# Moving the tiles that a matmul-bound kernel streams 128 bytes further on in SBUF

## Chip, cores and metric

One Trainium2 chip, one of its cores. The metric is the device time of one execution in microseconds (us): the median of the runs, beside one profiled execution whose span and trace are read below.

## What is computed

The input `x` has 4 sequences of 4096 tokens with 192 channels. A causal convolution of 7 taps runs over each channel (the taps are a softmax over `weight`, one row for each of 8 groups of channels), and its output goes through two feed-forward blocks of width 2048:

```python
a = conv(x, softmax(weight))                    # 16384 x 192
h = a @ w_in;   y = (h * cos(h)) @ w_out        # 192 -> 2048 -> 192
h = y @ w_in2;  g = h * clip(h + 3, 0, 6) / 6
out = g @ w_out2                                # 16384 x 192
```

## The kernel before

Everything is transposed: channels lie on the partitions, tokens along the free dimension. The tokens are cut into 32 blocks of 512 (`NB`, `N`), the width of 2048 into 16 chunks of 128 (`NJ`). One step `t` is one layer, one block and one chunk: `steps` lists 1024 of them.

To keep the precision of float32 with one-pass matmuls, every operand is split into a high part (rounded to `F32R`) and a remainder. A product is then three matmuls, high by high, high by low and low by high. `mm1` (line 622) makes `h` for two chunks at once: 9 products, each as two matmuls of 64 rows, one on partitions 0 to 63 and one on 64 to 127, which run side by side. Such a couple is called a pair below. `middle` (line 648) turns `h` into the activation and splits it into `gh` and `gl`; `mm2` (line 691) multiplies these by the second weights into the sums `a` and `b`, 5 pairs a step, one of them with 64 columns of weights only (`half_wide`, line 239). In all 9728 pairs run, 19456 of the 19564 matmul records. The other records are a warm-up in bfloat16 (line 767) and some of the convolutions, which run as float32 matmuls with diagonal weights (lines 484 and 500).

Every matmul loads its own weights, so a weight load (LDWEIGHTS) goes with each. Its **stationary** operand is a slice of `w0` or `w1`, the weights of a layer, which stay in SBUF throughout. Its **moving** operand, 512 columns of float32, is a half of `own`, `swap` or `last` (split input of a layer) or all of `gh` or `gl`.

The order of the work is a schedule computed ahead of the launch (`Schedule.place`) from costs and due times in the code; nothing in it depends on an address.

Where a tile lies follows from the pools, which stand one behind another in SBUF: `wpool` (the weights), `cpool` (constants and the diagonals), `raw_p` (weights being unpacked), `x_p`, `g_p`. Within a pool the tiles stand in the order in which the program first asks for them. In `x_p` that is `xb` (once), `xa` (twice), then `ta`, `tb`, `yb`, four `last`, four `own`, four `swap`, `ya`, `u`; in `g_p` it is `k`, `r`, `gh`, `gl`. The width of the first three is set by two constants, although only 518 columns of each are used:

```python
WIDE_A, WIDE_B = 520, 528                                       # line 43
v.data = new(v, x_p, F32, (P, WIDE_A))[:, : N + PAD]            # line 412, xa
v.data = new(v, x_p, F32, (P, WIDE_B))[:, : N + PAD]            # line 422, xb
```

With these widths the built program has these starts (bytes along a partition):

| tile | start | rest modulo 256 |
|---|---|---|
| `w0`, `w1` | 16512, 65664 | 128 |
| `diag0`, `diag1` | 114880, 118464 | 192 |
| `xb` | 134784 | 128 |
| `xa`, first and second | 136896, 138976 | 192, 224 |
| `last`, first of four | 147200 | 0 |
| `own`, first of four | 163584 | 0 |
| `swap`, first of four | 179968 | 0 |
| `gh`, first of four | 212736 | 0 |
| `gl`, first of four | 220928 | 0 |

All slices that the pairs take of a weight (512, 768, 1024 or 1536 bytes apart) and of a moving tile (2048 bytes apart) are whole multiples of 256 bytes from its start, so each of the 9728 pairs has moving operands with rest 0 and weights with rest 128.

Of the kernel before, what the change touches and what calls it, by code (L numbers as in the profile page):

```python
# [39 lines left out]
NW = 2 * D  # L40


WIDE_A, WIDE_B = 520, 528

UNBIAS_ON_ACT = 32
CAST_ON_ACT = 32
# [802 lines left out]
```

## Time and profile before

| | |
|---|---|
| median of 3 runs | 2318.5 us (2316.7 to 2319.52) |
| the profiled execution's own time | 2316.11 us |
| its span in the trace | 2314.3 us |
| granted TensorE clock, mean | 0.999 |
| PE busy | 2302.1 us, 99% of the span |
| PEld (weight loads) busy | 2066.3 us, 89% |
| DVE, ACT, POOL busy | 1729.7, 1688.6, 1412.2 us (75, 73, 61%) |

PE is TensorE's matmul, PEld its weight load, which overlaps with it. A matmul record lasts from its first column to its modelled end, so records overlap, and "PE busy" alone does not say how fast pairs follow one another. That is read from how many records start in a stretch of time, or from the starts in the timeline.

### The profile page before, as it was taken

How to read it: one execution, taken by the hardware profiler on the slowest of the kernel's cores; microseconds unless marked ns; L12 is line 12 of the kernel's file. 1: busy time of each engine (PE TensorE's matmuls, PEld its weight loads, DVE VectorE, ACT ScalarE, POOL GpSimd, SP SyncE). 2: the span in 40 equal slices, each digit the busy share in tenths (PEclk: the TensorE clock that was granted, in tenths of full speed). 3: DMA queues.
4: the chain of work that ended last, by engine and by line, in shares of the span. 5: the costliest groups of instructions: out<-in, count | busy, mean ns of one | idle time of the engine just before them, and what ended most of it. 6: DMA issues, size and time to landing. Idle time of an engine off the chain costs nothing.

```text
span 2314.3 us, 49748 instructions
## 1 busy us (share of the span) xinstructions
PE 2302.1 (99%) x19564; PEld 2066.3 (89%) x19564; DVE 1729.7 (75%) x2318; ACT 1688.6 (73%) x2977; POOL 1412.2 (61%) x1049
## 2 busy tenths in 40 slices
PE   9999999999999999999999999999999999999998
PEld 4888899999999999999999999999999999999998
DVE  8898976877768777678777778777687776875553
ACT  5998677776777777777767777777777677777675
POOL 2666666666656666666666666666666665665555
PEclk9999999999999999999999999999999999999999
DMA  5322211111101111101111011111011110111000
GB/s 150 84 67 54 55 41 26 45 40 28 44 19 38 40 33 40 37 20 40 39 38 35 26 31 44 38 31 40 18 44 40 30 43 22 26 35 33 17 22 14
DMA packets 39130, 90.91 MB, mean 39 GB/s; under 512 B 6256, under 2 KB 12400, under 8 KB 38896
## 3 DMA queue, kind: packets, MB, share of 16 engines
q1 hardware_dynamic: 38896, 87.74, 14.7%
q8 instruction: 153, 2.51, 0.4%
q14 instruction: 81, 0.66, 0.1%
HBM read 25.32 MB, written 12.58 MB: 16 GB/s over the span
## 4 chain that ended last, share of the span: by engine, by line
PE 98%; DVE 1%; ACT 0%; DMA 0%; SPq 0%; issue 0%; DVEq 0%; ACTq 0%
PE h L636 46%; PE a L705 31%; PE b L705 10%; PE b L242 10%; PE h L500 1%; DMA raw<-w 0%; ACT r L663 0%; ACT da L311 0%; DVE w L262 0%; DVE last L262 0%; ACT w L257 0%; DVE r L666 0%; DVE swap L262 0%; DVE swap L259 0%; ACT k L655 0%
## 5 line engine op out<-in xcount | busy, mean ns | idle before, releaser
L262 POOL TENSOR_TENSOR gl<-r,gh 128x512 fp32r<-128x512 f32 x1024 | 1396.5, 1377 | 866.3 <-ACT gh L257 772.6
L705 PE MATMUL a<-gh,w 64*128 64x512 f32 x4096 | 904.3, 392 | 0.2 <-DVE w L262 0.2
L636 PE MATMUL h<-own,w 64*128 64x512 f32 x3072 | 877.6, 392 | 0.7 <-ACT own L257 0.7
L636 PE MATMUL h<-swap,w 64*128 64x512 f32 x3072 | 665.1, 392 | 3.4 <-DVE swap L259 1.9
L705 PE MATMUL b<-gh,w 64*128 64x512 f32 x2048 | 666.2, 393 | 0.0
L242 PE MATMUL b<-gl,w 64*64 64x512 f32 x2048 | 662.9, 390 | 0.0
L705 PE MATMUL a<-gl,w 64*128 64x512 f32 x2048 | 662.7, 389 | 0.0
L705 PEld LDWEIGHTS a<-gh,w 64*128 64x128 f32 x4096 | 594.7, 185 | 65.5 <-ACT da L311 0.8
L257 ACT ACTIVATE gh<-r 128x512 fp32r<-128x512 f32 x1024 | 619.5, 631 | 32.4 <-DVE r L666 25.5
L636 PEld LDWEIGHTS h<-own,w 64*128 64x128 f32 x3072 | 568.0, 185 | 33.7 <-ACT own L257 1.5
L675 ACT ACTIVATE r<-h,three 128x512 f32<-128x512 f32 x512 | 324.8, 684 | 361.2 <-PE h L636 327.9
L636 PE MATMUL h<-last,w 64*128 64x512 f32 x3072 | 570.7, 391 | 0.0
L660 DVE SCALAR_TENSOR_TENSOR r<-k,h 128x512 f32<-128x512 int32 x512 | 334.9, 682 | 253.5 <-ACT k L655 134.3
L636 PEld LDWEIGHTS h<-swap,w 64*128 64x128 f32 x3072 | 489.6, 185 | 31.6 <-DVE swap L259 2.2
L678 DVE SCALAR_TENSOR_TENSOR r<-r,h 128x512 f32<-128x512 f32 x512 | 327.7, 679 | 219.1 <-ACT r L675 218.8
L636 PEld LDWEIGHTS h<-last,w 64*128 64x128 f32 x3072 | 407.8, 185 | 29.8
L655 ACT ACTIVATE k<-h 128x512 int32<-128x512 f32 x512 | 280.6, 594 | 171.8 <-PE h L636 171.1
L705 PEld LDWEIGHTS a<-gl,w 64*128 64x128 f32 x2048 | 375.9, 185 | 20.3 <-issue 0.8
L705 PEld LDWEIGHTS b<-gh,w 64*128 64x128 f32 x2048 | 376.2, 185 | 18.9 <-DVE tb L739 0.6
L666 DVE TENSOR_TENSOR r<-r,h 128x512 f32<-128x512 f32 x512 | 339.1, 684 | 52.1 <-ACT r L663 51.8
L663 ACT ACTIVATE r<-r,half_pi 128x512 f32<-128x512 f32 x512 | 353.7, 721 | 24.5 <-DVE r L660 23.6
L242 PEld LDWEIGHTS b<-gl,w 64*64 64x64 f32 x2048 | 268.3, 132 | 19.8
(70 smaller groups left out, 1123.7 us busy)
## 6 DMA issues: line engine op xcount, KB each, us to landing
swap<-own SPq DMA_DIRECT2D x126, 256.0 KB, 3.7
last<-last SPq DMA_DIRECT2D x64, 256.0 KB, 3.1
xa<-xa SPq DMA_DIRECT2D x32, 259.0 KB, 2.7
outT<-ta SPq DMA_DIRECT2D x32, 256.0 KB, 2.0
raw<-w SPq DMA_DIRECT2D x16, 384.0 KB, 3.3
xb<-xb SPq DMA_DIRECT2D x16, 259.0 KB, 2.6
raw<-w SPq DMA_DIRECT2D x32, 128.0 KB, 2.7
outT<-u SPq DMA_DIRECT2D x32, 128.0 KB, 2.3
```

The costliest lines, as they stand in the source:

```text
L242: pe.add_instruction(mybir.InstMatmult(name=nc.get_next_instruction_name(), engine=mybir.EngineType.PE, start_tensor_calc=False, stop_tens ...
L257: nc.scalar.activation(out=out, in_=in_, func=AF.Copy)
L262: (nc.vector if e == "dve" else nc.gpsimd).tensor_tensor(out, a, b, op=ALU.subtract)
L500: nc.tensor.matmul(y.data, lhsT=tap(i), rhs=x.data[:, i : i + N], start=(i == 0), stop=(i == TAPS - 1),)
L636: nc.tensor.matmul(h.data, lhsT=w[HALF[i], pw, c * P : (c + 1) * P], rhs=moving[i][c][HALF[i], px], start=(n == 0), stop=(n == len(passes) ...
L655: nc.scalar.activation(out=new(k, g_p, I32), in_=h.data, func=AF.Copy, bias=0.25, scale=1.0 / TWO_PI)
L660: nc.vector.scalar_tensor_tensor(new(r, g_p, F32), k.data, TWO_PI, h.data, ALU.mult, ALU.subtract)
L663: nc.scalar.activation(out=r.data, in_=r.data, func=AF.Sin, bias=half_pi, scale=-1.0)
L666: nc.vector.tensor_tensor(r.data, r.data, h.data, op=ALU.mult)
L675: nc.scalar.activation(out=new(r, g_p, F32), in_=h.data, func=AF.Relu, bias=three, scale=1.0)
L678: nc.vector.scalar_tensor_tensor(r.data, r.data, 6.0, h.data, ALU.min, ALU.mult)
L705: nc.tensor.matmul(out[i].data, lhsT=w_i, rhs=g.data[HALF[i]], **flags)
```

## The change

`xb` becomes 32 columns, 128 bytes, wider. The columns are not used; they push all that stands behind `xb` in `x_p` and `g_p` 128 bytes further on.

```diff
-WIDE_A, WIDE_B = 520, 528
+WIDE_A, WIDE_B = 520, 560
```

After it `own`, `swap`, `last`, `gh` and `gl` start with rest 128 modulo 256, as the weights do. `xb` and everything ahead of it stay. The instructions on each engine and their order are the same in both programs.

## Rows read from the trace of the kernel before

**Rows 1.** The page: busy time of each engine, and the granted clock in 40 slices.
```profile
PE 2302.1 (99%) x19564; PEld 2066.3 (89%) x19564; DVE 1729.7 (75%) x2318; ACT 1688.6 (73%) x2977; POOL 1412.2 (61%) x1049
PEclk9999999999999999999999999999999999999999
```
**Rows 2.** The page: the chain of work that ended last, by engine.
```profile
PE 98%; DVE 1%; ACT 0%; DMA 0%; SPq 0%; issue 0%; DVEq 0%; ACTq 0%
```
**Rows 3.** What PE waited for (engine line, awaited, us in total, times, longest).
```profile
PE h L636 <- DVE swap L259: 1.9, 1, 1.9
PE h L767 <- DVE w L796: 1.3, 1, 1.3
```
**Rows 4.** Stretches from 100 us on: length, busy us and count by engine, clock, DMA, GB/s.
```profile
100.00:500.00 400.00, 400.00 (x3444) 355.83 (x3442) 329.66 (x454) 307.70 (x550) 259.92 (x192) 1.00 0.20 51
500.00:1000.00 500.00, 500.00 (x4307) 456.72 (x4305) 377.05 (x482) 363.47 (x637) 309.68 (x227) 1.00 0.14 34
1000.00:1500.00 500.00, 500.00 (x4308) 456.75 (x4306) 381.74 (x489) 364.36 (x639) 310.43 (x227) 1.00 0.14 35
1500.00:2000.00 500.00, 500.00 (x4308) 456.83 (x4306) 379.39 (x488) 365.13 (x640) 309.69 (x227) 1.00 0.14 34
2000.00:2314.00 314.00, 308.39 (x2655) 281.18 (x2651) 175.35 (x247) 214.99 (x376) 183.62 (x140) 1.00 0.09 23
```
**Rows 5.** Timeline of PE: the bfloat16 warm-up (start us, us, engine, line, operation, count).
```profile
4.10 3.83 PE L767 MATMUL h<-w 128*128 128x512 bf16 x17
```
**Rows 6.** One line's instructions, 1000 to 1500 us: weight loads, ns min/median/max.
```profile
L636 PEld LDWEIGHTS h<-own,w x680: 184/184/188, 1000.5 to 1500.0; 64*128 64x128 f32 x170
...
L242 PEld LDWEIGHTS b<-gl,w x454: 131/131/135, 1002.8 to 1499.5; 64*64 64x64 f32 x152
```
**Rows 7.** Timeline of PE, 1016.90 to 1022.40 us.
```profile
1016.94 0.40 PE L705 MATMUL b<-gh,w 64*128 64x512 f32 x1
...
1017.18 0.39 PE L705 MATMUL a<-gl,w 64*128 64x512 f32 x1
...
1017.41 0.39 PE L242 MATMUL b<-gl,w 64*64 64x512 f32 x1
...
1018.35 0.39 PE L636 MATMUL h<-own,w 64*128 64x512 f32 x1
...
1018.58 0.40 PE L636 MATMUL h<-own,w 64*128 64x512 f32 x1
...
1018.82 0.39 PE L636 MATMUL h<-own,w 64*128 64x512 f32 x1
...
1020.91 0.39 PE L705 MATMUL a<-gh,w 64*128 64x512 f32 x1
...
1021.60 0.39 PE L705 MATMUL a<-gl,w 64*128 64x512 f32 x1
...
1022.05 0.39 PE L705 MATMUL a<-gh,w 64*128 64x512 f32 x1
...
1022.28 0.42 PE L705 MATMUL a<-gh,w 64*128 64x512 f32 x2
```
**Rows 8.** Timeline of the weight loads inside that stretch.
```profile
1018.35 0.18 PEld L636 LDWEIGHTS h<-own,w 64*128 64x128 f32 x1
1018.38 0.18 PEld L636 LDWEIGHTS h<-swap,w 64*128 64x128 f32 x1
1018.58 0.18 PEld L636 LDWEIGHTS h<-own,w 64*128 64x128 f32 x1
```
**Rows 9.** Weight loads by group, 1016.93 to 1017.18, then 1020.90 to 1022.30 us (busy, mean ns).
```profile
L705 PEld LDWEIGHTS a<-gl,w 64*128 64x128 f32 x1 | 0.2, 188 | 0.0
...
L705 PEld LDWEIGHTS a<-gh,w 64*128 64x128 f32 x6 | 0.8, 184 | 0.1
```
**Rows 10.** Timeline of PE: the convolution of `xb` with `diag1`, then of `xa` with `diag0`.
```profile
39.52 6.28 PE L500 MATMUL h<-xb,diag 128*128 128x512 f32 x14
...
46.63 6.28 PE L500 MATMUL h<-xa,diag 128*128 128x512 f32 x14
```

## The prediction

> **What bounds the kernel now.** I read the busy times and the granted clock first. PE is busy for 2302.1 of 2314.3 us and the clock stands at its upper level, 2.4 GHz, in all 40 slices [rows 1]. The chain that ended last is 98% PE [rows 2], and the list of waits says that PE hardly ever stood still for anybody: its longest wait in the whole run is 1.9 us, and the next 1.3 us [rows 3]. So the time is the number of matmul pairs times the spacing of pairs, plus a start of some 100 us in which the first weights and blocks arrive.
>
> The spacing comes from the stretches. Between 1000 and 1500 us 4308 matmul records start [rows 4], which is 2154 pairs, 232.1 ns each; the other stretches give the same. From 100 us to the end the counts are 3444 + 4307 + 4308 + 4308 + 2655 = 19,022 records, **9511 pairs** [rows 4]. Each nanosecond of the spacing is therefore worth 9.5 us of the run.
>
> Is 232.1 ns all streaming? The bfloat16 warm-up has the same 512 columns: 17 records in 3.83 us, of which the last lasts 0.38, so (3.83 - 0.38) / 16 = 215.6 ns each [rows 5]. A pair thus spends 16.5 ns more than columns alone ask for, and it is these 16.5 ns that an address could touch. They are not constant. In the timeline the first halves of eight consecutive pairs start between 1016.94 and 1018.82 us, 235 ns apart, and some 2 us later those of six pairs start between 1020.91 and 1022.28, 228.3 ns apart [rows 7]. The pair at 1016.94 is followed after 0.24 us, and the two between 1021.60 and 1022.05 take 0.225 each, to the timeline's 10 ns. Same kind of instruction, same clock, no wait. Something inside TensorE's reads varies, and there is one trace of it: a weight load takes 184 ns and now and then 188, one of 64 columns 131 and now and then 135 [rows 6], and the load that ran beside the long pair at 1016.94 is one of 188 ns [rows 9]. Weight load and matmul get in each other's way there.
>
> **The change part by part.** No instruction is added, removed or reordered. Three things move.
>
> *The moving operands of all 9728 pairs.* They start 128 bytes apart from the weights modulo 256 before, and 0 apart after. I work out what that does if the two reads disturb each other when they stand at the same rest modulo 256. The next weight load starts with the matmul: matmul at 1018.35, load at 1018.35; at 1018.58 both again [rows 7, 8]. Halving the columns shortens a load by 184 - 131 = 53 ns [rows 6], so a column of weights takes 0.83 ns and 128 of them are read in 107 ns, 4.8 bytes a ns on each partition. The matmul reads 2048 bytes in some 216 to 232 ns, 8.8 to 9.5 bytes a ns. It gains 4 to 4.7 bytes a ns on the load: one lap of 256 bytes in 55 to 64 ns. Before, the load starts half a lap ahead; it is overtaken after about 30 ns and again after about 85 to 95 ns, twice within its 107 ns. After, the two start level, the matmul draws ahead, and it comes round once, after 55 to 64 ns; the second lap would end at 109 ns or later, when the load has read all. One meeting fewer in each pair, if the start itself is not one.
>
> What a meeting costs stands in no row by itself. Bounds: all 16.5 ns could be such meetings, and all could go (215.6 ns a pair: 16.5 x 9511 = 157 us less); or the start becomes a third meeting and all pairs are as long as the one at 1016.94 (240 ns: 7.9 x 9511 = 75 us more). Two meetings in 16.5 ns would be 8 ns each, so that one fewer would give 224 ns. I take less, **228 ns**, because six pairs in a row already run at that spacing today [rows 7], with loads of 184 ns that were not lengthened [rows 9]: it is a speed that the trace shows, where 224 is a division. The gain is (232.1 - 228) x 9511 = **39 us**.
>
> *`xa` and the tiles of the other engines.* `ta`, `yb`, `k`, `r` and the rest move together by the same 128 bytes, so their places to one another stay. DVE and ACT are busy for 381.74 and 364.36 of 500 us [rows 4]; if PE needs 2% less time they stand at 78 and 74%, and POOL at 63%. That cover remains, and I cost them at nothing; without it, 2% longer operations there would still be hidden behind PE. The transfers into these tiles have the same number and size; the DMA share is 0.14 [rows 4]. What would be late next is nothing that I can name.
>
> *The matmuls of the convolutions.* They are 84 of 19,564 records, and lie ahead of 52 us; nothing.
>
> The sum: 2316.1 us for the profiled execution, less 39, is 2277. The median of the runs lies 2.4 us above the profiled execution, so I predict **2279 us**.
>
> **The rivals.**
>
> *Slower: level at the start is the worst place.* Matmul and load begin within 10 ns of each other [rows 7, 8]. With equal rests they then ask for the same place at once, every time, and if the matmul does not draw ahead at once, the start is a meeting that no phase can avoid. It decides from the point at which a pair's average meetings go above today's, that is when the collision at the start costs more than the meeting that falls away. If every second pair became long, as in the stretch from 1016.94 to 1018.82, the spacing would be 235: 2.9 x 9511 = 28 us more, 2346 us. If all did: 240 ns, 2394 us. For it: loads of 188 ns do go with a long pair [rows 9]. Against it: beside the pair at 1017.18 runs a load of half as many columns, that of line 242 for the pair at 1017.41, and it takes 0.23 us like the mean [rows 7]. So the cost now seems to sit in the first half of a load, where the meeting after 30 ns is, and this one goes.
>
> *No change: the addresses do not matter.* Before, two convolutions run with different distances: `xb` with rest 128 against a diagonal with 192, and `xa` (its first buffer) with rest 192 against 192, which is the level case. Both take 6.28 us for 14 records [rows 10]. That is the same to 10 ns, on the same engine. Against it: these are float32 matmuls over all 128 rows, at 0.43 us or so a record, with one load in that time where the pairs have one in 0.23; they may leave room that the pairs do not have. The 16.5 ns could belong to this type of matmul. Then the time stays at 2318.5 us. The Trainium skill says so as a rule ("SBUF — State Buffer", section Who interferes with whom): TensorE has two read ports that are independent, one for the moving operand and one for weight loads, and it never waits on anyone. By that rule the sum is zero; the load of 188 ns beside the long pair is where this trace does not agree.
>
> *The change does not do what it says.* Only what stands behind `xb` moves. The starts of the tiles say that it does for all five moving tiles, so this is left with next to nothing and is counted with no change.
>
> **How the numbers follow.** About 0.2% (4.6 us, half a nanosecond a pair) is what a measurement of this kernel can tell from no change. Faster: 0.57, because the meetings are in the trace and the count of them falls; its own range is 2230 us (223 ns a pair) to 2310 (231). No change: 0.19. Slower: 0.24, most of it between 2325 and 2350 us, the rest up to 2394. The likeliest is faster, at 2279. The range reaches from 2230, below which I leave some 0.08 (towards the bound of 215.6 ns, 2162 us), to 2348, above which some 0.11 is left.
>
> **What would show it.** Right: 1000 to 1500 us holds about 4386 matmul records (500 us over 228 ns, twice) at a clock of 1.00, PE's waits stay at a few us, loads of 188 ns get rare, and the whole gain is spread evenly over the run from 100 us on. The rival of the level start: fewer than 4308 records there, the median load above 184 ns. No change: 4308 within 10. The prediction is wrong if the spacing goes up, or if it goes down and a wait of PE on DVE or ACT gives it back.

## The result, and the profile after

The changed kernel takes **2283.77 us** (median of 4 runs, 2283.35 to 2284.76), the kernel before 2317.6 us in the runs beside it (2316.41 to 2319.52). The ratio is 0.9854, 95% interval 0.9837 to 0.9871: 33.8 us less. Forecast were 2279 us, with a range from 2230 to 2348. The profiled execution took 2284.76 us, with a span of 2283.0 us, against 2314.3 before.

The page of the changed kernel, busy times and granted clock, answers to [rows 1]:

```profile
PE 2271.2 (99%) x19564; PEld 2033.0 (89%) x19564; DVE 1725.4 (76%) x2318; ACT 1689.7 (74%) x2977; POOL 1411.3 (62%) x1049
...
PEclk9999999999999999999999999999999999999999
```

PE is still busy for all but 12 us of the span. A digit 9 of the clock says that a slice, some 57 us, had 90% or more of the upper level of 2.4 GHz on average, as in the kernel before; that the upper level held in the bulk of the run is read from the stretches below, at 1.00. No instruction went away: 19,564 matmul records, as before. The chain that ended last answers to [rows 2], and the list of what PE waited for to [rows 3] (engine line, awaited, us in total, times, longest):

```profile
PE 98%; DVE 1%; ACT 1%; issue 0%; POOL 0%; DVEq 0%; POOLq 0%; ACTq 0%
```

```profile
PE h L636 <- DVE swap L259: 1.8, 1, 1.8
PE h L767 <- DVE w L796: 1.3, 1, 1.3
```

The two longest waits are the same two, within 0.1 us. So the gain came out of no wait, and no new one took it back. It is in how fast pairs follow one another, and that is read from the stretches, which answer to [rows 4]; the first 100 us stand here too (length, then busy us and count of PE, PEld, DVE, ACT, POOL, clock, DMA share, GB/s):

```profile
0.00:100.00 100.00, 94.45 (x545) 59.31 (x547) 86.85 (x162) 71.47 (x137) 37.45 (x38) 0.97 0.40 114
100.00:500.00 400.00, 399.68 (x3492) 341.42 (x3490) 332.70 (x458) 311.53 (x557) 264.25 (x195) 1.00 0.20 51
500.00:1000.00 500.00, 500.00 (x4374) 426.88 (x4372) 382.87 (x494) 371.77 (x651) 313.68 (x230) 1.00 0.14 35
1000.00:1500.00 500.00, 500.00 (x4375) 436.53 (x4372) 382.76 (x493) 370.56 (x649) 314.50 (x231) 1.00 0.14 35
1500.00:2000.00 500.00, 500.00 (x4374) 492.40 (x4373) 382.23 (x493) 369.72 (x646) 315.28 (x231) 1.00 0.14 34
2000.00:2283.00 283.00, 277.02 (x2421) 276.49 (x2417) 157.94 (x220) 194.64 (x340) 166.16 (x128) 0.99 0.10 25
```

The count of PE is what matters. Between 1000 and 1500 us 4375 records start where 4308 did: 2187.5 pairs, 228.6 ns each, where they had 232.1. The three stretches of 500 us agree to one record, so the gain is even over the run. Times the 9511 pairs of the prediction, (232.13 - 228.57) x 9511 = 33.8 us, which is the difference of the medians. The two profiled executions differ by a little less, 31.3 us of span; the first 100 us are part of that, since 545 records start there after the change and 559 before, seven pairs or 1.6 us. The clock is not the same in that start: from 25 to 30 us the granted share was 0.50 (the lower level, 1.2 GHz) after the change, with 22 records, and 0.71 before, with 33. The whole stretch before the change:

```profile
0.00:100.00 100.00, 93.74 (x559) 58.93 (x561) 86.48 (x163) 72.95 (x140) 38.88 (x38) 0.98 0.41 115
```

PEld's busy time says nothing here: 426.88, 436.53 and 492.40 us go with one and the same spacing. Loads of the two halves overlap, and where they overlap more, their union is shorter.

A line's weight loads between 1000 and 1500 us (ns min/median/max), to be laid beside [rows 6]:

```profile
L636 PEld LDWEIGHTS h<-own,w x690: 182/184/185, 1001.9 to 1498.9; 64*128 64x128 f32 x173
...
L242 PEld LDWEIGHTS b<-gl,w x460: 131/131/132, 1000.1 to 1499.8; 64*64 64x64 f32 x154
```

The longest loads of these two groups have gone, 188 to 185 and 135 to 132 ns; the median stays.

The timeline of PE (start us, us, engine, line, operation, operands, number of records merged into the row), at the start of a `mm1` and at the start of the `mm2` behind it, answers to [rows 7]:

```profile
1002.16 0.61 PE L636 MATMUL h<-own,w 64*128 64x512 f32 x2
...
1003.75 0.62 PE L636 MATMUL h<-last,w 64*128 64x512 f32 x4
1004.20 0.39 PE L705 MATMUL a<-gl,w 64*128 64x512 f32 x1
1004.21 0.39 PE L636 MATMUL h<-last,w 64*128 64x512 f32 x1
```

`mm1` has nine pairs. The first half of its first one starts at 1002.16, that of the first pair of `mm2` at 1004.20: 2.04 us, 227 ns a pair. Means over the starts of all first halves, from the 800th to the 9300th pair, tell the two products apart: `mm1` went from 232.4 to 226.85 ns, `mm2` from 232.25 to 230.5. With 4608 pairs of the one and 5120 of the other that is 25.6 + 9.0 = 34.6 us, three quarters of it in `mm1`. In what follows "spacing of `mm1`" and "of `mm2`" are these means.

### The profile page after: what moved, and what is told of

It reads as the page before. It is cut to its first block, busy times and chain, and to the rows that moved or that the text cites. A ratio compares the mean times of both kernels' runs of the same rounds, so it can differ in the third digit from the quotient of the medians.

```text
span 2283.0 us, 49748 instructions
## 1 busy us (share of the span) xinstructions
PE 2271.2 (99%) x19564; PEld 2033.0 (89%) x19564; DVE 1725.4 (76%) x2318; ACT 1689.7 (74%) x2977; POOL 1411.3 (62%) x1049
## 4 chain that ended last, share of the span: by engine, by line
PE 98%; DVE 1%; ACT 1%; issue 0%; POOL 0%; DVEq 0%; POOLq 0%; ACTq 0%
PE h L636 45%; PE a L705 30%; PE b L242 12%; PE b L705 10%; PE h L500 1%; PE h L767 0%; PE h L484 0%; ACT k L655 0%; ACT gh L257 0%; DVE r L666 0%; DVE r L660 0%; ACT r L663 0%; DVE da L322 0%; DVE swap L259 0%; DVE swap L262 0%
## 5 line engine op out<-in xcount | busy, mean ns | idle before, releaser
L636 PE MATMUL h<-own,w 64*128 64x512 f32 x3072 | 862.2, 387 | 0.7 <-ACT own L257 0.7
L705 PE MATMUL b<-gh,w 64*128 64x512 f32 x2048 | 658.8, 390 | 0.0
L705 PE MATMUL a<-gl,w 64*128 64x512 f32 x2048 | 654.9, 386 | 0.3 <-POOL gl L262 0.3
L636 PE MATMUL h<-swap,w 64*128 64x512 f32 x3072 | 651.9, 387 | 3.0 <-DVE swap L259 1.8
L705 PEld LDWEIGHTS a<-gh,w 64*128 64x128 f32 x4096 | 602.7, 184 | 53.6 <-DVE ta L739 1.0
L257 ACT ACTIVATE gh<-r 128x512 fp32r<-128x512 f32 x1024 | 621.5, 630 | 32.4 <-DVE r L666 25.6
L636 PE MATMUL h<-last,w 64*128 64x512 f32 x3072 | 560.1, 386 | 0.0
L636 PEld LDWEIGHTS h<-swap,w 64*128 64x128 f32 x3072 | 478.3, 185 | 37.2 <-DVE swap L259 2.1
```

Source lines behind the costliest of these rows:

```text
L257: nc.scalar.activation(out=out, in_=in_, func=AF.Copy)
L636: nc.tensor.matmul(h.data, lhsT=w[HALF[i], pw, c * P : (c + 1) * P], rhs=moving[i][c][HALF[i], px], start=(n == 0), stop=(n == len(passes) ...
L705: nc.tensor.matmul(out[i].data, lhsT=w_i, rhs=g.data[HALF[i]], **flags)
```

## The experiments

All were timed beside the kernel before on the same chip, which took 2316.4 to 2316.6 us each time. "Distance" is the start of the weights less that of the moving operand, modulo 256: 128 before, 0 after. Each fence holds the stretch from 1000 to 1500 us in the columns of the view above; the count of PE, the first in brackets, gives the spacing (1000 us over the count).

### Whose address is it?

The theory: the distance of moving operands to weights, in which the two reads meet. The rivals: the absolute place of the moving tiles, or that of the tiles of the other engines that moved along.

**1. Weights moved by 128 bytes as well**, and so everything behind them (against the kernel before, with `xb` as wide as it was there). `own`, `swap`, `last`, `gh`, `gl` and all other tiles behind `xb` lie where the change has them, but the distance is 128 again.

```diff
+pad = wpool.tile([P, 32], F32, tag="pad", name="pad")
 W = [wpool.tile([P, NJ, 2, NW], F32R, tag=f"w{l}", name=f"w{l}") for l in range(2)]
```

> The weights and everything behind them lie 128 bytes further on than in the kernel before, so that the moving operands lie exactly where the changed kernel has them (own at 163712), but half a lap of 256 bytes from the weights again. If the distance between the two operands decides: as before, 2318 us, 4308 records from 1000 to 1500 us. If the place of the moving operands themselves, or of the tiles of the other engines, decides: as the change, 2284 us, 4375 records.

```profile
1000.00:1500.00 500.00, 500.00 (x4308) 443.91 (x4306) 381.87 (x489) 364.33 (x640) 310.07 (x227) 1.00 0.14 35
```

2316.32 us, ratio 1.0 (0.999 to 1.0009), and 4308 records, the very count of before. The whole gain is gone.

**2. Only the weights moved.** `xb` gets 8 columns less and two small scratch tiles are saved, so that `own`, `gh` and the rest stay at the addresses of before; weights at rest 0, moving operands at rest 0 (against the kernel before).

```diff
-WIDE_A, WIDE_B = 520, 528
+WIDE_A, WIDE_B = 520, 520
...
-half_pi = cpool.tile([P, 1], F32, tag="half_pi", name="half_pi")
-three = cpool.tile([P, 1], F32, tag="three", name="three")
+both = cpool.tile([P, 2], F32, tag="both", name="both")
+half_pi, three = both[:, :1], both[:, 1:]
...
+pad = wpool.tile([P, 32], F32, tag="pad", name="pad")
...
-kf, sm = t("skf", I32), t("ssum", m=1)
+kf, sm = k, t("ssum", m=1)
```

> Only the weights move by 128 bytes; own, swap, last, gh and gl stay where the kernel before has them (own at 163584), and so do all tiles of x_p and g_p but xb. Distance 0 modulo 256. If the distance decides: as the change, 2284 us. If the place of the moving operands or of the other engines' tiles decides: as before, 2318 us.

```profile
1000.00:1500.00 500.00, 500.00 (x4374) 497.77 (x4372) 382.16 (x492) 370.57 (x650) 315.39 (x231) 1.00 0.14 35
```

2283.83 us, 0.9857 (0.9843 to 0.9872): the whole gain, with no moving tile touched.

**3. The same without the pad** (against experiment 2): weights where they were, moving operands 128 bytes to the other side, 256 bytes below those of the change.

```diff
-pad = wpool.tile([P, 32], F32, tag="pad", name="pad")
```

> The moving operands lie 128 bytes further back instead of further on (own at 163456); the weights stay. Distance 0 modulo 256, but 256 bytes from that of the change modulo 512. If the lap is 256 bytes long: as the change, 2284 us. If it is 512 bytes or longer: another time, 2318 us or something beyond either; the distances of both kernels modulo 512 would then already have differed among the weights' own slices, so I give this little chance.

```profile
1000.00:1500.00 500.00, 500.00 (x4374) 441.12 (x4372) 382.16 (x492) 370.54 (x650) 315.18 (x231) 1.00 0.14 35
```

2283.55 us, 0.9859 (0.9844 to 0.9874). 128 bytes down do what 128 bytes up do, as a period of 256 wants it. Together the three settle whose address it is: experiment 1 against the change, and experiment 2 against before, differ in the distance, and the time follows the distance each time. By rests modulo 256 of weights and moving operands, 128 and 128 (the change) and 0 and 0 (experiment 2) are fast, 128 and 0 (before) and 0 and 128 (experiment 1) are not.

**4. Only `gh` and `gl` moved**, the operands of `mm2` (against the kernel before). If each pair paid for its own distance alone, the pairs of `mm2` would give their share and `mm1` nothing.

```diff
-WU = {}
+WU, pad = {}, g_p.tile([P, 32], F32, tag="pad", name="pad", bufs=1)
```

> Only gh and gl (the pairs of the second product, 5120 of 9728) lie 128 bytes further on; own, swap and last stay. If each pair gains by its own distance, in equal parts: 34 us x 5120/9728 = 18 us, 2300 us. If the gain of a pair depends on what the pairs before left behind: less or more than that, and the other half of the change makes up the rest. If the gain came from the split inputs alone: 2318 us.

```profile
1000.00:1500.00 500.00, 500.00 (x4316) 406.32 (x4314) 382.72 (x491) 365.30 (x641) 311.06 (x227) 1.00 0.14 35
```

2312.1 us, 0.9982 (0.9973 to 0.9991): 4 us, a quarter of what an equal share of all pairs would be. `mm1` stands at 232.6 ns, `mm2` at 231.2; the 230.5 that `mm2` has in the change it does not reach with the same distance. That is a first sign that a pair's spacing hangs on the pairs around it too.

### Do laps explain it? The other distances

The prediction counted how often the matmul's read meets the load's read: twice at distance 128, once at 0. That makes forecasts for the distances between. All four runs change the width of `xb` alone, against the kernel before; experiments 5 and 6 have the distance 32 and 64, experiments 7 and 8 go past level to 224 and 192. The width of `xb` is 552 in experiment 5, as shown, and 544, 568 and 576 in the next three.

```diff
-WIDE_A, WIDE_B = 520, 528
+WIDE_A, WIDE_B = 520, 552
```

> xb is 552 columns wide, so the weights lie 32 bytes ahead of the moving operands modulo 256 (before: 128, change: 0). By laps: the matmul gains 4 to 4.7 bytes a ns, overtakes the load after 7 to 8 ns and again after 61 to 72 ns, both inside the 107 ns of the load: two meetings as before, 2318 us. If nearness to the change's place is enough: 2284 us or little above.

> xb is 544 columns wide: the weights lie 64 bytes ahead. By laps: overtaken after about 15 ns and 75 ns, two meetings, 2318 us. If the time changes evenly with the distance: half way, 2301 us.

> xb is 568 columns wide: the weights lie 32 bytes behind the moving operands. By laps: the matmul is ahead, comes round after 48 to 56 ns and again after 102 to 120 ns, when the load has read all or nearly all: one meeting, and none at the start, so 2284 us or less. If only the level place is good: 2300 us or more.

> xb is 576 columns wide: the weights lie 64 bytes behind (192 ahead). By laps: the matmul comes round after 41 to 48 ns and again after 95 to 112 ns, so one meeting and often a second: between 2284 and 2318 us.

Experiment 5, distance 32:

```profile
1000.00:1500.00 500.00, 500.00 (x4301) 491.13 (x4300) 381.42 (x487) 363.20 (x637) 310.06 (x227) 1.00 0.14 35
```

Experiment 6, distance 64:

```profile
1000.00:1500.00 500.00, 500.00 (x4288) 401.05 (x4286) 380.95 (x486) 360.92 (x633) 309.20 (x226) 1.00 0.14 35
```

Experiment 7, distance 224:

```profile
1000.00:1500.00 500.00, 500.00 (x4292) 454.67 (x4290) 381.17 (x486) 361.57 (x634) 309.74 (x227) 1.00 0.14 35
```

Experiment 8, distance 192:

```profile
1000.00:1500.00 500.00, 500.00 (x4374) 438.31 (x4372) 383.32 (x493) 370.64 (x649) 315.41 (x231) 1.00 0.14 35
```

| distance | layout | median, us | ratio (95%) | spacing of `mm1`, `mm2`, ns |
|---|---|---|---|---|
| 0 | the change | 2283.77 | 0.9854 (0.9837 to 0.9871) | 226.85, 230.5 |
| 32 | experiment 5 | 2320.22 | 1.0015 (1.0006 to 1.0025) | 233.0, 232.5 |
| 64 | experiment 6 | 2325.99 | 1.0041 (1.0027 to 1.0055) | 233.5, 233.15 |
| 128 | before | 2316.4 to 2317.6 | 1 | 232.4, 232.25 |
| 192 | experiment 8 | 2284.33 | 0.9862 (0.9848 to 0.9877) | 228.9, 228.7 |
| 224 | experiment 7 | 2325.4 | 1.0038 (1.0023 to 1.0053) | 233.4, 233.0 |

The laps fall with experiment 7: at 224 they left one late meeting, and wanted 2284 us or less. It took 2325.4. Two distances are good, 0 and 192, and the one between them is among the worst. The spacing of `mm1` and `mm2` also shows that 0 and 192 are not the same state: the totals agree, the shares do not.

The weight loads of experiment 6, to be laid beside [rows 6]:

```profile
L636 PEld LDWEIGHTS h<-own,w x678: 183/184/185, 1000.5 to 1498.4; 64*128 64x128 f32 x170
```

The slowest layout of all has no load of 188 ns either. Of 7604 loads of 128 columns between the 800th and the 9300th pair, 950 last 187 ns or more before (one in eight, and the pairs beside which they run take 240.8 ns on average), none do in the change, and none in experiment 6. So lengthened loads mark one of the slow patterns. They do not measure the loss: the other pairs of the kernel before take 231.3 ns on average, so the long loads go with about 1 of the 3.5 ns.

### Distance alone?

**9. Distance 0, at another place**: weights and moving operands both 32 bytes further on (against the changed kernel).

```diff
+pad = wpool.tile([P, 8], F32, tag="pad", name="pad")
 W = [wpool.tile([P, NJ, 2, NW], F32R, tag=f"w{l}", name=f"w{l}") for l in range(2)]
```

> The weights lie 32 bytes and the moving operands 160 bytes further on than in the kernel before: distance 0 as in the change, but both 32 bytes off the multiples of 64 on which all fast kernels so far have their moving operands. If the distance alone decides: as the change, 2284 us. If the two slower runs at 32 bytes ahead and behind were slow because the moving operands lay at 32 modulo 64: slower, 2320 to 2326 us like those.

```profile
1000.00:1500.00 500.00, 500.00 (x4374) 413.15 (x4372) 382.05 (x493) 370.55 (x649) 315.18 (x231) 1.00 0.14 35
```

2284.06 us, 0.9853 (0.9839 to 0.9868), with the spacings of the change to 0.01 ns. Four layouts have the distance 0 by now, and lie within 0.6 us.

**10. The best of both**: `mm1` at distance 0 as in the change (226.85 ns), `mm2` at 192 as in experiment 8 (228.7 ns). If the spacings add up, it beats both (against the changed kernel).

```diff
-WU = {}
+WU, pad = {}, g_p.tile([P, 16], F32, tag="pad", name="pad", bufs=1)
```

> own, swap and last at distance 0 as in the change, where the trace shows the pairs of the first product at 226.9 ns; gh and gl at 64 bytes behind (weights behind), where the pairs of the second product take 228.7 ns against 230.5 in the change. If a pair's spacing is set by its own distance: 4608 x 226.9 + 5120 x 228.7 against 4608 x 226.9 + 5120 x 230.5 ns, 9 us less than the change, 2275 us, faster than both kernels. If it also hangs on the pairs before it (half of the change, gh and gl alone, gave 4 us where its share was 18): 2284 us or more.

```profile
1000.00:1500.00 500.00, 500.00 (x4356) 413.30 (x4354) 383.46 (x494) 369.75 (x649) 313.52 (x230) 1.00 0.14 36
```

2292.83 us, 0.9892 (0.9878 to 0.9907): 9 us slower than the change, where it was to be faster. `mm2` stayed at 230.5, and `mm1`, whose weights and moving tiles lie at the very addresses of the change, went to 229.0. That is (229.0 - 226.85) x 4608 = 9.9 us, all that was lost.

The trace shows where in `mm1` it was lost. The starts of the first halves of its first pair, its sixth, and the first pair of the `mm2` behind it:

```profile
1010.66 0.39 PE L636 MATMUL h<-own,w 64*128 64x512 f32 x1
...
1011.82 0.39 PE L636 MATMUL h<-swap,w 64*128 64x512 f32 x1
...
1012.73 0.39 PE L705 MATMUL a<-gl,w 64*128 64x512 f32 x1
```

Five pairs take 1.16 us, 232 ns each; the last four take 0.91 us, 227 ns each. Over 390 `mm1` that follow an `mm2` directly, the first five pairs take 230.6, 235.4, 228.7, 231.7 and 230.2 ns on average and each of the last four 226.7, the pace of the change. Where an `mm1` follows another `mm1` (56 of them), all nine positions lie between 226.7 and 227.6. A pair's spacing therefore hangs on the distance in the pairs before it as well as on its own, and at this distance the disturbance is gone after five pairs.

### Is it the length of the load?

**11. Fewer weight columns at the distance of before**: seven of the nine pairs of `mm1` load 32 columns in place of 128, and leave out the rest of their products (against the kernel before). If the load's reads are what costs, less to read costs less.

```diff
                 for i, h in enumerate(hs):
+                    if n % 8:
+                        half_wide(h.data[:32], w[HALF[i], pw, c * P : c * P + 32], moving[i][c][HALF[i], px])
+                        continue
```

> The layout of the kernel before, but 7 of the 9 pairs of the first product load only the first 32 columns of their weights and add to the first 32 rows of h alone, so most of the three-part product is left out. The load then reads for 27 ns instead of 107, and by laps the matmul overtakes it after 30 ns at the earliest, so never. If the loads cause all that a pair takes above 215.6 ns: those 3584 pairs at 216, 232.4 - 216 = 16 ns x 3584 = 59 us less, 2259 us. If they cause only what the change took away and the rest belongs to this type of matmul: 226 to 227 ns there, about 21 us less, 2296 us. If the loads have nothing to do with it: 2317 us.

```profile
1000.00:1500.00 500.00, 500.00 (x4302) 397.16 (x4300) 381.58 (x487) 363.74 (x637) 310.38 (x227) 1.00 0.14 35
```

Its short loads, of line 242, in the same stretch:

```profile
L242 PEld LDWEIGHTS h<-own,w x565: 102/104/108, 1002.1 to 1498.3; 64*32 64x32 f32 x189
```

The loads are shorter by 184 - 104 = 80 ns, and the time is 2319.37 us, 1.0009 (1.0 to 1.0019). `mm1` moves by half a nanosecond (231.9), `mm2` loses one (233.2).

**12. The same at distance 0** (experiment 11 with the width of the change).

```diff
-WIDE_A, WIDE_B = 520, 528
+WIDE_A, WIDE_B = 520, 560
```

> The changed kernel with the same narrow loads: 7 of the 9 pairs of the first product load 32 columns of weights only and add to 32 rows of h, most of the three-part product is left out. With narrow loads the layout of before stayed at 2319 us, so laps are out. If the effect of the distance sits in the first 32 columns of a load, near its start: 2284 us, give or take 5, as with whole loads. If it needs the rest of the load: the gain of the first product (4608 pairs, 232.4 to 226.9 ns, 25 of the 34 us) is lost for 7 of 9 pairs, 2300 us or more.

```profile
1000.00:1500.00 500.00, 500.00 (x4330) 355.23 (x4328) 384.22 (x494) 368.16 (x646) 310.75 (x228) 1.00 0.14 36
```

2305.61 us, 0.9953 (0.9936 to 0.9969). `mm2`, whose loads are untouched, has about the spacing of the change (230.1 ns). `mm1` with its short loads stands at 232.05, as at distance 128, and not at 226.85: it takes five nanoseconds a pair **more** with 32 columns than with 128. So the gain of `mm1` is no matter of less reading in the way of the matmul. What it needs these two runs do not separate: the narrow pairs also write 32 rows of `h` in place of 128, and loads of two lengths follow one another. The change shows the same on a small scale: in its `mm2` the one pair with weights of 64 columns (`b<-gl`) is the longest of the five, 235.8 ns on average, where it took 231.0 before.

No run beat the change; experiment 8 equals it within its interval.

## Why the prediction was right, and where not

*What bounds the kernel.* Right, but for a detail: the digits of [rows 1] do not show the upper level of the clock "in all 40 slices", since the granted share was 0.71 from 25 to 30 us; the sum starts at 100 us and is not touched by it. The spacing of pairs sets the time, at 9.5 us for each nanosecond: 3.56 ns gave 33.8 us. That PE spends more than the 215.6 ns of its columns [rows 5], and that these are what an address can touch, held in every run: the layouts span 228.6 to 233.2 ns at a clock of 1.00, with PE busy for the whole of the 500 us.

*The size.* The term was (232.1 - 228) x 9511 = 39 us, with 228 taken from six pairs in a row that already ran at 228.3 [rows 7]. It measured 228.6 ns, and the count of records in the stretch 4375 for the 4386 announced; the 4.8 us between 2279 and 2283.77 are this half nanosecond. The value was a good one and partly luck: it is the mean of two products that went to 226.85 and 230.5, which nothing in the rows of before foretold.

*The sign's reason.* Here a step failed: "One meeting fewer in each pair, if the start itself is not one". The lap arithmetic is refuted by experiment 7, which by it was to be as good as the change and came out at 2325.4 us, by experiment 11, where the load read only 32 columns and nothing was gained, and by experiment 12, where less reading at distance 0 cost 22 us. With the reason gone, the right sign was luck as well: the same arithmetic promised as much for 224, which is slower than before. What the runs put in its place is narrower: the time depends on the distance of weights to moving operand, 0 and 192 are good, 32, 64, 128 and 224 are not, and the pairs before have a say. What couples the two inside TensorE was not settled.

*The sign that was to show it.* Loads of 188 ns did get rare, as announced. But experiment 6 has none and is the slowest, so this sign would have confirmed a wrong layout too. The count of records is the sign to trust.

*The other engines' tiles, priced at nothing.* Right. DVE, ACT and POOL were busy for 382.76, 370.56 and 314.50 of 500 us, 77, 74 and 63%, and the waits of PE stayed at 1.8 and 1.3 us. Experiment 2, which leaves these tiles of `x_p` and `g_p` where they were, has the same time as the change.

*The rivals.* "Level at the start is the worst place" is refuted at distance 0. Its outcome exists, though: 32, 64 and 224 are slower than before, by up to 9.4 us, which is far less than the 28 and 75 us that it was given, since even in experiment 6 pairs of 240 ns do not come one after another: the longest there took 236. "The addresses do not matter" is refuted by experiments 1 and 2. The two convolutions of equal length [rows 10] were bad evidence for it: float32 matmuls over 128 rows at two distances said nothing of 64-row pairs with a load in each. By the rule of the Trainium skill ("SBUF — State Buffer", section Who interferes with whom), under which TensorE's two reads are independent, the sum was zero. This case does not agree: experiment 2 against before measures 32.7 us, and the measurement decides.

*What stays open.* Why pairs at another distance disturb the five pairs of `mm1` behind them in experiment 10, and those of `mm2` in the change hardly do; why 192 and 0 are good and 224 between them is not; and what makes up the 13 ns by which the best layouts still exceed the 215.6 ns of the warm-up. Distances between the multiples of 32, 96 and 160 were not tried.

## What to carry to other kernels

Where TensorE is busy all the time and waits for nobody, compare the spacing of its matmuls with that of a plain run of the same columns; if something is left, sweep the distance between the tiles of weights and of moving operands in steps of 32 bytes, which costs a few columns of padding. Measure each step and the whole kernel: neither a neighbouring distance nor the sum of two separate gains foretold the time here. Before trusting a sign in the trace (here, lengthened weight loads), see that a slow layout really shows it.

## What was not expected of the hardware

- Padding alone is worth 1.8% of this kernel, from 2283.6 to 2326.0 us, in steps: the layouts at distance 0 and 192 near 2284, the others between 2316 and 2326, and nothing between until the two products were given different distances (2292.8 and 2312.1).
- Less weight to load made pairs slower: at distance 0, `mm1` takes 226.85 ns a pair with loads of 184 ns and 232.05 when most of them are of 104 ns.
- The two halves of a pair need not run side by side, and how far apart they run does not set the spacing. In the changed kernel the second half of the last pair of `mm1` starts at 1004.21 us, behind the first half of the next pair at 1004.20 (the last two rows of the timeline above): the halves are a whole pair apart. In experiment 5 the second half of a pair starts 0.22 us behind the first early in the run and 0.03 us behind it late (first pair of a `mm1`, first half and second half):

```profile
401.05 0.39 PE L636 MATMUL h<-own,w 64*128 64x512 f32 x1
401.27 0.39 PE L636 MATMUL h<-swap,w 64*128 64x512 f32 x1
...
1802.71 0.39 PE L636 MATMUL h<-own,w 64*128 64x512 f32 x1
1802.74 0.39 PE L636 MATMUL h<-swap,w 64*128 64x512 f32 x1
```

  Yet its three stretches of 500 us from 500 us on count 4301, 4301 and 4300 records. So a meeting of the reads of the two halves is not what makes pairs long or short.
